# Attention with beacons, then a squared-ReLU feed-forward: fp32 loads and casting transfers at the start, and half products for one more chunk

## The chip, the cores and the metric

The kernel runs on one core of one Trainium2 chip. The metric is the device time of one execution in microseconds (us). Before the change it is 328.27 us, the median of 3 runs that lie between 327.58 and 329.05.

A core has five engines that run their own programs side by side: TensorE (PE; its weight loads are listed apart as PEld), VectorE (DVE), ScalarE (ACT), GpSimd (POOL) and SyncE (SP). SP, ACT and POOL issue transfers here: SP's and ACT's go through hardware queues, POOL's through the software queue, which can also convert fp32 to bf16 on the way.

## The reference

```python
scores = scale * np.matmul(q, k_all.transpose(0, 1, 3, 2))   # k_all = [beacon_k ; k]
scores = np.where(causal, -1000000000.0, scores)             # beacons are always seen
a = np.exp(scores - scores.max(-1, keepdims=True))
a /= a.sum(-1, keepdims=True) + 1e-09
x = np.matmul(a, v_all)                                      # v_all = [beacon_v ; v]
...
h = np.maximum(x @ w_in, 0.0)
return ((h * h) @ w_out).astype(np.float32)
```

There are 8 batches of 8 heads, 576 tokens and 16 beacons for each batch, 64 elements a head. The attention's result, transposed to 4608 tokens of 512, goes through w_in (512 x 2048) and w_out (2048 x 512). Inputs and output are fp32; the kernel computes in bf16 with fp32 sums.

## The kernel before

**Two streams on one TensorE.** Attention runs batch by batch, two heads (a pair) at a time: scores into two wide PSUM strips (names `qk`, line 650), exponentials on ScalarE (`exp`, lines 672 and 748), causal masks on VectorE (`mask`, with the table `tri`), products with v (`av`, line 793), division (`norm`, line 812), and a transpose into xT (`xtp`, `xte`, later `xt` by DMA). The feed-forward runs in nine chunks of 512 tokens, behind the attention: `s1.chunk.part` (line 1095, 512-column matmuls into the PSUM tiles ps), `relu` and `sq` on ScalarE or VectorE, and the second product.

**The second product has two forms.** Chunks 0 and 1 (`j < FAST`, FAST is 2) take the plain one, `s2.chunk.group.quarter` on line 1145: four token groups, four quarters of w_out, 16 matmuls of 512 columns for each group. Chunks from 2 on take the form with seven products on line 1204: the four quadrants of g and of w_out are combined, seven products of halves are made in place of eight (each 2 x 8 matmuls of 256 columns), and VectorE builds sums of quadrants ahead of them (`sum`, line 1176, eight a chunk) and adds the products up behind them (`ev`). Four sums of w_out's quadrants (`wsum`) are made once.

**The order is a table.** SEQUENCE lists every operation by name, with the engine behind an @ where there is a choice (A, D, P). An engine's program is its own operations in the table's order; nothing is reordered when it runs. Buffers (two strips, four ps tiles, six fp32 staging tiles `stg`) are handed out in that order too.

**The start.** Batch 0's tokens 0 to 239 of q and k come in fp32 through hardware queues into osb (`fldq`, `fldk`: pair 0, pair 1, pairs 2 and 3; k's issued by SP, q's by ScalarE) and are cast and paired (`fcq`, `fck`). Its tokens 240 to 575 (part 1) come through the software queue, cast on the way (`sld0..1`, line 474), and VectorE or GpSimd copies two heads side by side (`two0.1.pair`). TensorE transposes pairs (`tp`, line 512), VectorE or ScalarE moves them to qT and kT (`eq`, `ek`, lines 354 and 352). Batch 1's q and k come the same way as part 1 (`sld1`, `two1.0`). The beacon rows of k go through a stg tile (`bkl`, `bkc`). v of batches 0 and 1 comes in fp32 through the software queue into stg (`ld0v`, `ld1v`, line 399) and GpSimd or VectorE casts it to vb (`cast0v`, `cast1v`, line 354). The same queue then carries w_in and w_out in quarters (`win`, line 885; `wout`, line 893), cast on the way. Later batches load q, k and v in fp32 through SP into stg; GpSimd casts.

**Fills.** `fill` is a matmul of the identity with itself (line 486) into a free ps tile; its result is never read. There are 16 of 512 columns, all in the first microseconds or among batch 0's work.

Of the kernel before, what the change touches and what calls it, by code (L numbers as in the profile page):

```python
# [16 lines left out]
fldq2 fcq2@D ld0v3 ident fill6 fill5 fill10 fill15 fldq1 sld0q1.0 fill3 fldq0 sld0k1.0 fill12 fcq3@A fcq1 tp0.0.3q  # L17
eq0.0.3@A tpg0.0.3q fldk1 fck1 tp0.0.1k ek0.0.1@D tpg0.0.1k tri sld0q1.2 tp0.0.2q eq0.0.2@D tpg0.0.2q fill2 fldk2
fill11 fcq0 tp0.0.0q fck2 tp0.0.2k fill4 ek0.0.2@A tpg0.0.2k bkl0 bkc0 tpb0 tp0.0.1q sld0k1.2 fill13 eq0.0.0@A
tpg0.0.0q eq0.0.1@A ekb0 tpg0.0.1q qk2.0.0 exp2.0.0 qk1.0.0 exp1.0.0 two0.1.1q@D tp0.1.1q fck3 tp0.0.3k ek0.0.3@A  # L20
two0.1.0k@D fldk0 fill7 tpg0.0.3k fck0 tp0.0.0k ek0.0.0@A two0.1.1k@D sld1q0.0 tp0.1.1k eq0.1.1@D ek0.1.1@A qk3.0.0
two0.1.0q@D tp0.1.0q tpg0.0.0k qk1.1.1 tpg0.1.1q ld0v0 tp0.1.0k mask1.0.0 ld0v1 tpg0.1.1k fill9 exp3.0.0 ld0v2
exp1.1.1 eq0.1.0@A tpg0.1.0q two0.1.3k@D ek0.1.0@D tpg0.1.0k qk0.0.0 exp0.0.0 sld1k0.2 mask2.0.0 cast0v3 two1.0.1q@D
mask0.0.0 sld1k0.0 qk1.1.0 exp1.1.0 fill8 two0.1.3q@P tp0.1.3q eq0.1.3@D qk0.1.0 ld0v4 qk0.1.2 mask1.1.0 win0
cast0v0@D exp0.1.0 exp0.1.2 tp1.0.1q eq1.0.1@D tpg1.0.1q win1 qk1.1.2 exp1.1.2 tpg0.1.3q cast0v1@P av1.0.0 norm1.0.0
ld1v1 tp0.1.3k qk0.1.1 exp0.1.1 ek0.1.3@A av2.0.0 norm2.0.0 two0.1.2q@P tpg0.1.3k tp0.1.2q mask1.1.1 two0.1.2k@D
tp0.1.2k eq0.1.2@A ek0.1.2@A tpg0.1.2q sld1q0.2 win3 win2 cast0v2 qk3.1.0 exp3.1.0 mask3.0.0 bkl1 bkc1 two1.0.0q@D
tpg0.1.2k av0.0.0 cast0v4 norm0.0.0 qk2.1.0 fill0 av3.0.0 exp2.1.0 xtp0.0.1 xtp0.0.0 qk3.1.1 exp3.1.1 xte0.0.1@D
xte0.0.0@D tpb1 ekb1 fill1 qk3.1.2 norm3.0.0 xtp0.0.2 xte0.0.2@D exp3.1.2 mask0.1.0 mask0.1.1 av1.1.0 norm1.1.0
qk2.1.2 exp2.1.2 mask3.1.1 fill14 tp1.0.0q eq1.0.0@A tpg1.0.0q ld1v3 two1.0.0k@P mask3.1.0 av0.1.0 xtp0.0.3 xte0.0.3@A  # L30
tp1.0.0k qk2.1.1 av3.1.0 norm0.1.0 exp2.1.1 xtp0.1.0 ld1v4 xte0.1.0@A s1.0.0.0 ek1.0.0 tpg1.0.0k qk4.2 relu0.0.0@A
warm wout1 norm3.1.0 mask2.1.0 mask2.1.1 two1.0.1k@P wout3 two1.0.2q@P tp1.0.1k ek1.0.1 tpg1.0.1k exp4.2.1.0.0
s1.0.1.0 relu0.1.0@D xtp0.1.3 av2.1.0 s1.0.2.0 xte0.1.3@D relu0.2.0@D ld2k0 exp4.2.0.0.0 s1.0.4.0 relu0.4.0@D
norm2.1.0 s1.0.3.0 relu0.3.0@A tp1.0.2q eq1.0.2@A tpg1.0.2q xtp0.1.1 xte0.1.1@D qk4.4 xtp0.1.2 xte0.1.2@A s1.0.5.0
relu0.5.0@D two1.0.2k@P tp1.0.2k exp4.4.1.0.0 s1.0.7.0 ek1.0.2 relu0.7.0@A ld1v2 s1.0.6.0 relu0.6.0@A mask4.0.0
tpg1.0.2k sq0.1.0@D s1.0.1.1 relu0.1.1@D ld1v0 cast1v3 s1.0.0.1 two1.0.3k@D exp4.4.0.0.0 mask4.0.2 relu0.0.1@A
s1.0.5.1 relu0.5.1@A s1.0.3.1 relu0.3.1@A qk5.7 exp5.7.-1.1.0 s1.0.15.1 relu0.15.1@A two1.0.3q@P exp5.7.1.0.0
s1.0.12.1 relu0.12.1@D s1.0.4.1 relu0.4.1@D wout0 s1.0.10.0 exp5.7.-1.0.0 s1.0.14.0 relu0.14.0@A s1.0.7.1 relu0.7.1@A
relu0.10.0@D s1.0.2.1 relu0.2.1@A cast1v1 exp5.7.0.0.0 s1.0.15.0 relu0.15.0@D wout2 sq0.7.0@A s1.0.14.1 relu0.14.1@D
s1.0.11.1 relu0.11.1@D sq0.7.1@A s1.0.9.0 relu0.9.0@A s1.0.8.0 s1.0.6.1 s1.0.13.0 relu0.6.1@A mask4.0.1 relu0.8.0@D  # L40
# [12 lines left out]
qk8.4 exp8.4.1.0.0 exp8.4.0.0.0 relu1.9.0@D tr3q st0 s1.1.14.0 relu1.14.0@D tr3k ld3v0 cast3v0 ld3v1 cast3v1 s1.1.13.0
s1.1.2.0 relu1.2.0@A ld3v2 qk8.2 relu1.13.0@D cast3v2 ld3v3 ld3v4 ld4k0 cast3v4 ld4q0 exp8.2.0.0.0 cast4k0
exp8.2.1.0.0 s1.1.15.0 relu1.15.0@D mask8.0.1 mask8.0.0 s1.1.1.0 wsum1 relu1.1.0@A s1.1.3.0 s1.1.7.0 relu1.3.0@A
s1.1.4.0 relu1.4.0@D ld4q1 s1.1.12.0 sq1.1.0@D mask8.0.2 s1.1.0.0 cast4q0 s1.1.6.0 cast3v3 cast4q1 ld4q2 ld4q3 ld4k1
ld4q4 cast4q3 cast4q4 relu1.0.0@A sq1.0.0@D relu1.7.0@A relu1.12.0@D relu1.6.0@A s1.1.8.0 relu1.8.0@A s1.1.5.0
relu1.5.0@D cast4q2 cast4k1 av8.0.0 ld4k2 sq1.3.0@A ld4k3 norm8.0.0 qk9.7 ld4k4 cast4k4 sq1.6.0@A exp9.7.-1.1.0
av8.0.1 norm8.0.1 s1.1.10.0 exp9.7.1.0.0 exp9.7.1.0.1 relu1.10.0@D sq1.2.0@D s1.1.11.0 exp9.7.-1.0.0 s2.1.1.0
mask9.0.0 relu1.11.0@D exp9.7.0.0.0 s2.1.0.0 sq1.4.0@A qk10.10 exp10.10.-1.1.0 exp10.10.0.0.0 exp10.10.1.0.0 mask9.0.2  # L60
sq1.5.0@D exp10.10.-1.0.0 s2.1.1.1 s2.1.0.1 s2.1.1.2 s2.1.0.2 qk11.13 exp11.13.-1.0.0 exp11.13.-1.1.0 cast4k3
sq1.7.0@D s2.1.0.3 mask9.0.1 ev1.0@A s2.1.1.3 s2.1.2.0 ev1.1@A st2 mask10.0.2 mask10.0.1 mask10.0.0 av10.0.0
norm10.0.0 s2.1.2.1 exp11.13.0.0.0 xtp2.0.0 xte2.0.0@A av10.0.1 norm10.0.1 av9.0.0 norm9.0.0 s2.1.2.2 xtp2.0.2 tr4q
# [147 lines left out]
def kernel(  # L211
# [29 lines left out]
    def sb(name, shape, dt):  # L241
        return pool.tile(shape, dt, name=name)

    FAST = 2
    BOTH = 7
    NSTG, NPT, RB = 6, 3, 3
    NFILL = 16
# [1114 lines left out]
```

## Time and profile before

| | before |
|---|---|
| median of 3 runs | 328.27 us |
| the profiled execution | 326.74 us |
| its span, first to last instruction | 325.0 us |
| granted TensorE clock, mean | 0.994 of full speed |
| TensorE instructions | 3428 matmuls, as many weight loads |

The span holds all engines' work; 1.7 us of the execution's time lie outside it. The page of the profile gives each engine's busy time as a share of the span and as a strip of 40 digits, each a slice of 8.1 us (9: busy 90% or more). Views of the trace behind it list groups of equal instructions by source line, waits and what ended them, and single instructions with their start in us from the span's begin. In rows of the kind "29.1, 454 | 0.9 <-PE" stand the busy time of the group, the mean of one in ns, and the idle time of the engine just ahead of them with what ended it.

### The profile page before, as it was taken

How to read it: one execution, taken by the hardware profiler on the slowest of the kernel's cores; microseconds unless marked ns; L12 is line 12 of the kernel's file. 1: busy time of each engine (PE TensorE's matmuls, PEld its weight loads, DVE VectorE, ACT ScalarE, POOL GpSimd, SP SyncE). 2: the span in 40 equal slices, each digit the busy share in tenths (PEclk: the TensorE clock that was granted, in tenths of full speed). 3: DMA queues.
4: the chain of work that ended last, by engine and by line, in shares of the span. 5: the costliest groups of instructions: out<-in, count | busy, mean ns of one | idle time of the engine just before them, and what ended most of it. 6: DMA issues, size and time to landing. Idle time of an engine off the chain costs nothing.

```text
span 325.0 us, 8419 instructions
## 1 busy us (share of the span) xinstructions
PE 314.7 (97%) x3428; PEld 225.4 (69%) x3428; DVE 234.9 (72%) x495; ACT 224.7 (69%) x332; POOL 105.2 (32%) x157
## 2 busy tenths in 40 slices
PE   5889999999999999999999999999999999999995
PEld 2458875645465548878886476657878788888884
DVE  2798493648727888558876778659977597988872
ACT  3897995555867896667765588567874874985920
POOL 8997534327406802422334024413000340000000
PEclk9799999999999999999999999999999999999999
DMA  7999999989999999799988998999520510030033
GB/s 164 213 205 224 230 216 196 184 175 244 217 215 204 222 218 209 144 225 185 206 190 188 205 189 193 169 170 225 125 44 2 141 63 0 2 114 17 3 129 131
DMA packets 145601, 51.97 MB, mean 160 GB/s; under 512 B 132506, under 2 KB 140570, under 8 KB 145562
## 3 DMA queue, kind: packets, MB, share of 16 engines
q1 hardware_dynamic: 135901, 42.32, 63.3%
q0 software_dynamic: 8512, 8.49, 15.2%
q10 hardware_dynamic: 1149, 0.62, 0.8%
q8 instruction: 27, 0.44, 0.6%
q14 instruction: 12, 0.10, 0.1%
HBM read 37.22 MB, written 9.44 MB: 144 GB/s over the span
## 4 chain that ended last, share of the span: by engine, by line
PE 93%; DVE 2%; DMA 2%; issue 1%; ACT 0%; POOL 0%; DVEq 0%; POOLq 0%
PE ps L1095 30%; PE ps L1204 25%; PE ps L793 9%; PE ps L1145 9%; PE strip L650 6%; PE strip L972 4%; PE ps L972 3%; PE strip L1204 2%; PE ps L650 2%; DMA qk_area<-in_q_dram 2%; PE ps L512 1%; PE ps L861 1%; PE ps L486 0%; DVE xn L812 0%; DVE qT L354 0%
## 5 line engine op out<-in xcount | busy, mean ns | idle before, releaser
L1095 PE MATMUL ps<-xT,w_in 128*128 128x512 bf16 (+6 forms) x640 | 104.3, 315 | 0.2 <-issue 0.2
L1095 PEld LDWEIGHTS <-w_in 128*128 128x128 bf16 x640 | 57.2, 98 | 35.4 <-issue 1.7
L748 ACT ACTIVATE pt<-strip 128x1024 bf16<-128x1024 f32 (+3 forms) x77 | 70.2, 952 | 10.1 <-PE strip L650 9.9
L354 POOL CAST qk_area<-stg 128x512 bf16<-128x512 f32 (+2 forms) x60 | 41.2, 712 | 48.7 <-DMA stg<-in_k_dram 24.9
L1110 ACT ACTIVATE g<-ps 128x512 bf16<-128x512 f32 (+2 forms) x74 | 39.0, 551 | 21.7 <-PE ps L1095 18.9
L354 POOL CAST vb<-stg 128x512 bf16<-128x512 f32 (+1 forms) x39 | 27.7, 722 | 76.6 <-DMA stg<-in_v_dram 76.6
L1204 PEld LDWEIGHTS <-g 128*128 128x128 bf16 x448 | 42.7, 98 | 6.7 <-issue 1.1
L1112 DVE TENSOR_SCALAR g<-ps 128x512 bf16<-128x512 f32 (+2 forms) x54 | 32.8, 614 | 20.0 <-PE ps L1095 17.3
L771 DVE TENSOR_TENSOR pt<-pt,tri 128x512 bf16<-128x512 bf16 (+1 forms) x93 | 35.8, 410 | 8.3 <-ACT pt L748 7.9
L793 PEld LDWEIGHTS <-pt 128*128 128x128 bf16 x930 | 34.9, 99 | 6.2 <-issue 1.2
L1204 PE MATMUL ps<-w_out,g 128*128 128x256 bf16 x304 | 38.0, 273 | 0.0
L793 PE MATMUL ps<-vb,pt 128*128 128x65 bf16 x930 | 37.6, 194 | 0.2 <-DVE vb L354 0.2
L1204 PEld LDWEIGHTS <-sum_area 128*128 128x128 bf16 x336 | 31.8, 98 | 5.6 <-issue 1.0
L812 DVE TENSOR_TENSOR xn<-ps,rcp 128x320 bf16<-128x320 f32 (+2 forms) x64 | 31.5, 492 | 2.2
L1120 ACT ACTIVATE g<-g 128x1024 bf16<-128x1024 bf16 (+2 forms) x31 | 28.4, 944 | 5.6 <-DVE g L1112 5.3
L748 ACT ACTIVATE pt<-ps 128x512 bf16<-128x512 f32 x42 | 23.7, 598 | 11.6 <-PE ps L650 11.4
L1145 PE MATMUL ps<-w_out,g 128*128 128x512 bf16 x128 | 31.1, 379 | 0.0
L810 DVE RECIPROCAL rcp<-ps 128x5 f32<-128x5 f32 (+2 forms) x64 | 12.1, 189 | 24.8 <-PE ps L793 24.0
L352 ACT COPY osb<-ps 128x512 f32<-128x512 f32 x24 | 14.1, 590 | 20.9 <-PE ps L1204 16.2
L650 PE MATMUL strip<-qT,kT 64*128 64x128 bf16 (+15 forms) x406 | 27.5, 256 | 0.6 <-ACT pt L672 0.6
L650 PEld LDWEIGHTS <-kT 64*128 64x128 bf16 x520 | 17.5, 95 | 14.2 <-issue 9.4
L1204 PE MATMUL ps<-w_sum,sum_area 128*128 128x256 bf16 x208 | 27.0, 273 | 0.0
(100 smaller groups left out, 383.5 us busy)
## 6 DMA issues: line engine op xcount, KB each, us to landing
out_dram<-osb SPq DMA_DIRECT2D x16, 512.0 KB, 3.9
stg<-in_q_dram SPq DMA_DIRECT2D x24, 256.0 KB, 4.9
stg<-in_k_dram SPq DMA_DIRECT2D x18, 256.0 KB, 4.5
stg<-in_v_dram SPq DMA_DIRECT2D x18, 256.0 KB, 5.6
w_in<-in_moe_w_in_dram POOLq DMA_DIRECT2D x4, 512.0 KB, 12.0
w_out<-in_moe_w_out_dram POOLq DMA_DIRECT2D x4, 512.0 KB, 12.1
stg<-in_v_dram POOLq DMA_DIRECT2D x6, 256.0 KB, 9.1
stg<-in_k_dram SPq DMA_DIRECT2D x6, 224.0 KB, 3.8
```

Of the source, the lines that this page charges most:

```text
L354: eng[e].tensor_copy(dst, src)
L650: nc.tensor.matmul(out, kT[b % 2][hp, pr, 128 * c:128 * c + 128], rhs, start=True, stop=True)
L748: nc.scalar.activation(out, in_, AF.Exp, bias=0.0, scale=scale)
L771: nc.vector.tensor_tensor(out=d, in0=d, in1=tri[0:rows, m0:m0 + m, 0:w][:, None].to_broadcast([rows, 2, m, w]), op=ALU.min)
L793: nc.tensor.matmul(a[0:w, at + (t - tl[0]) * (D + 1):at + (t - tl[0] + 1) * (D + 1)], P[0:rr, hj, o:o + w], vb[b % 2][0:rr, c, 2 * pr + hj ...
L812: nc.vector.tensor_tensor(out=xn[b % 2].rearrange("p t (h d) -> p h t d", d=D)[:, h0:h0 + nh, tl[0]:tl[0] + nt], in0=a[:, :, :, 0:D], in1= ...
L1095: nc.tensor.matmul(h[:, lo - spans[0][0]:hi - spans[0][0]], w_in_sb[:, mc, ft * 128:(ft + 1) * 128], xT[:, mc, lo % RING:lo % RING + hi - lo],
L1110: nc.scalar.activation(dst, h, AF.Relu, bias=0.0, scale=1.0)
L1112: nc.vector.tensor_scalar(out=dst, in0=h, scalar1=0.0, scalar2=None, op0=ALU.max)
L1120: nc.scalar.activation(d, d, AF.Square, bias=0.0, scale=1.0)
L1145: nc.tensor.matmul(o, G[:, fc, ts * 128:(ts + 1) * 128], w_out_sb[:, fc, :], start=(fc == 0), stop=(fc == NFT - 1))
L1204: nc.tensor.matmul(o, lhs[:, f, t * 128:(t + 1) * 128], rhs[:, f], start=fresh and f == 0, stop=f == HF - 1, skip_group_check=True)
```

## The change

- FAST goes from 2 to 1: chunk 1's second product is made by seven half products, with its eight sums; the four `wsum` stand ahead of it in one block.
- Batch 0's part 1 of q and k is loaded in fp32 through hardware queues into stg (`rldk0` by ScalarE, `rldq0`, `rldq2`, `rldk2` by SP). The pairing copies read it there and cast; seven of the eight stand on GpSimd, one on VectorE. All eight of batch 1's stand on GpSimd too.
- v of batches 0 and 1 is cast by the software queue's transfer and lands in vb itself; its staging tiles and its ten casts go (nine on GpSimd, one on VectorE).
- The beacon rows of k land in g[0], and chunk 0's first four relus of each pass wait for their cast.
- Fills: 32 of 256 columns. 19 stand in the start, 4 around the end of chunk 0's first product, 8 in the stretch of chunk 1's second product, 1 near the end.
- `tri` has two tiles in place of four (three were alike).
- SEQUENCE is another order throughout; batch 2's first load stands behind batch 0's pairings.

```diff
-fldq2 fcq2@D ld0v3 ident fill6 fill5 fill10 fill15 fldq1 sld0q1.0 fill3 fldq0 sld0k1.0 fill12 fcq3@A fcq1 tp0.0.3q
...
+bkl0 fldq1 ident tri fill6 fill2 fill1 fill28 fill16 fill15 fill25 ld0v0 bkc0 tpb0 fldk1 bkl1 fck1 tp0.0.1k fill5
+fill4 fldq2 fcq3@D ek0.0.1@D tpg0.0.1k tp0.0.3q fill29 bkc1 ekb0 ld0v1 eq0.0.3@D tpg0.0.3q fcq1 tp0.0.1q eq0.0.1@D
+sld1q0.0 fldq0 fill24 ld0v4 fill27 qk1.0.0 tpg0.0.1q fldk2 fck2 tp0.0.2k fck3 rldk0@A ld0v3 fcq2@A fldk0 ek0.0.2@D
...
-    FAST = 2
+    FAST = 1
...
-    NFILL = 16
+    NFILL = 32
...
-        for i in range(4):
+        for i in range(2):
...
         def emit_load(e):
-            st = stg[ld.held[1]]
+            st = vb[b % 2][:, c, :, 0:D] if soft else stg[ld.held[1]]
...
         ld = add(f"ld{b}{x}{c}", "POOL" if soft else "SP", (1.35 if soft else 1.0) if lo else (0.9 if soft else 0.65), emit_load,
-                 take=("stg", 1), dma=1.2 * rows / 128, behind=[] if soft else load_chain[-1:] + behind, sync=sync)
+                 take=None if soft else ("stg", 1), dma=1.2 * rows / 128, behind=[] if soft else load_chain[-1:] + behind, sync=sync)
...
             load_chain.append(ld)
+        else:
+            cast[b, x, c] = ld
+            return
...
     def add_beacon(b):
+        raw = g[0].rearrange("p f t -> p (f t)")[0:Nb, b * 2 * H * D:(b + 1) * 2 * H * D].bitcast(FP32).rearrange(
+            "p (h d) -> p h d", h=H)
         ld = add(f"bkl{b}", "SP", 0.45, lambda e: [nc.sync.dma_start(
-            out=stg[ld.held[1]][0:Nb], in_=beacon_k[b].transpose([1, 0, 2]))], dma=0.1,
-                 deps=[bk_ev[b - 1]] if b else [], take=("stg", 1))
-        bk = add(f"bkc{b}", "DVE", 0.4, lambda e: nc.vector.tensor_copy(bks[b % 2], stg[ld.held[1]][0:Nb]), deps=[ld], give=ld)
+            out=raw, in_=beacon_k[b].transpose([1, 0, 2]))], dma=0.1)
+        bk = add(f"bkc{b}", "DVE", 0.4, lambda e: nc.vector.tensor_copy(bks[b % 2], raw), deps=[ld] + ([tpb_ops[b - 1]] if b else []))
         cast[b, "bk"] = bk
         box = {}
...
-        box["t"] = add(f"tpb{b}", "PE", 0.2, emit_tp, deps=[bk, ident_op], take=("ps", 1))
+        box["t"] = tpb_ops[b] = add(f"tpb{b}", "PE", 0.2, emit_tp, deps=[bk, ident_op], take=("ps", 1))
...
-    bk_ev = {}
+    bk_ev, tpb_ops = {}, {}
+
+    def raw_part(x):
+        _, np_, ns = parts_of[0][1]
+        n = "qk".index(x) * NSTG // 2
+        return stg_all[0:np_, n:n + NSTG // 2].rearrange("p a b -> p (a b)").rearrange("p (h s d) -> p h s d", h=H, s=ns)
+
+    def add_raw_loads():
+        t0, np_, ns = parts_of[0][1]
+        for lo in range(0, HP, HP // 2):
+            for x, t in (("k", k), ("q", q)):
+                h = slice(2 * lo, 2 * lo + HP)
+
+                def emit(e, t=t, x=x, h=h):
+                    return [eng[e].dma_start(
+                        out=raw_part(x)[:, h],
+                        in_=t[0, h, t0:t0 + np_ * ns, :].rearrange("h (p s) d -> p h s d", s=ns))]
+
+                o = add(f"rld{x}{lo}", ("SP", "ACT"), {"SP": 0.45, "ACT": 0.55}, emit, dma=1.04)
+                for pr in range(lo, lo + HP // 2):
+                    strided[0, 1, pr, x] = o
...
     def add_fill(i):
         def emit(e):
-            nc.tensor.matmul(ps[fill.held[1]], ident, ident[:, None, :].to_broadcast([128, 4, 128]), start=True, stop=True)
-
-        fill = add(f"fill{i}", "PE", 0.216, emit, deps=[ident_op], take=("ps", 1))
+            nc.tensor.matmul(ps[fill.held[1]][:, 0:256], ident, ident[:, None, :].to_broadcast([128, 2, 128]), start=True, stop=True)
+
+        fill = add(f"fill{i}", "PE", 0.108, emit, deps=[ident_op], take=("ps", 1))
         fill.give = [fill]
...
         if b > 0:
-            after = [w_ops["in", 3]] if b == 1 else [strided[b - 1, 0, HP - 1, "q"]]
-            add_part_loads(b, 0, after, free)
+            add_part_loads(b, 0, None, free)
...
                             copy_on(e, paired_buf(b, x, part)[:, pr].rearrange("p s (u d) -> p u s d", u=2),
-                                    strided_buf(b, x, part)[:, 2 * pr:2 * pr + 2])
+                                    (strided_buf(b, x, part) if b else raw_part(x))[:, 2 * pr:2 * pr + 2])
 
                         joined[b, part, pr, xs] = add(f"two{b}.{part}.{pr}{xs}", ("DVE", "POOL"),
-                                                      {"DVE": 0.14 + 2 * ns * D / 3000.0, "POOL": 0.15 + 2 * ns * D / 850.0},
+                                                      {"DVE": 0.14 + 2 * ns * D / (3000.0 if b else 1400.0), "POOL": 0.15 + 2 * ns * D / (1100.0 if b else 850.0)},
                                                       emit_pair, deps=[strided[b, part, pr, xs]])
...
                     relus.append(add(f"relu{j}.{ft}.{n}", ("ACT", "DVE"), {"ACT": 0.17 + N / 1200.0, "DVE": 0.157 + N / 960.0},
-                                     emit_relu, deps=[s1] + (tp_ops[0, 1] if j == 1 else []), give=s1))
+                                     emit_relu, deps=[s1] + (tp_ops[0, 1] if j == 1 else [])
+                                     + ([cast[i, "bk"] for i in range(NPE)] if j == 0 and ft < 4 * NPE // 2 else []), give=s1))
 
...
                 add_fill(i)
-            part_loads = add_part_loads(0, 1, [tri_op], [])
+            add_raw_loads()
...
             behind, sync = [], []
-            if x == "v" and b == 0:
-                if c == 0:
-                    behind = part_loads
-            elif x == "v" and b == 1 and c == 0:
-                behind = [strided[1, 0, HP - 1, "q"]]
-            elif b == 2 and n == 0:
+            if b == 2 and n == 0:
                 sync = [w_ops["out", 3]]
+                behind = [joined[0, 1, pr, y] for pr in range(HP) for y in "kq"]
...
```

Where the table moves things, shown as the instructions of one engine in program order (source line, operation, tile written and tiles read, shape):

**GpSimd, early program, from the loads of batch 0's late q and k to the first weights.** Before:

```order
L474 DMA qk_area<-in_q_dram 112x4x192
L474 DMA qk_area<-in_k_dram 112x4x192
L474 DMA qk_area<-in_q_dram 96x4x384
L398 DMA stg<-in_beacon_v_dram 16x8x64
L399 DMA stg<-in_v_dram 112x8x64
L399 DMA stg<-in_v_dram 128x8x64 x2
L474 DMA qk_area<-in_k_dram 96x4x384
L354 CAST vb_66<-stg 128x8x64
L474 DMA qk_area<-in_k_dram 96x4x384
L354 COPY g_81<-qk_area 112x2x3x64
L399 DMA stg<-in_v_dram 80x8x64
L885 DMA w_in<-in_moe_w_in_dram 128x4x512 x2
```

After:

```order
L399 DMA vb_66<-in_beacon_v_dram 16x8x64
L400 DMA vb_66<-in_v_dram 112x8x64
L400 DMA vb_66<-in_v_dram 128x8x64
L499 DMA qk_area<-in_q_dram 96x4x384
L400 DMA vb_66<-in_v_dram 80x8x64
L400 DMA vb_66<-in_v_dram 128x8x64 x2
L499 DMA qk_area<-in_k_dram 96x4x384
L355 CAST g_81<-stg 112x2x3x64 x2
L909 DMA w_in<-in_moe_w_in_dram 128x4x512
L355 CAST g_81<-stg 112x2x3x64 x4
L355 COPY w_sum<-qk_area 96x2x6x64 x2
L355 CAST g_81<-stg 112x2x3x64
```

The loads of the late q and k have left this engine (rows of 112 partitions on line 474), v is written to vb straight, and the pairings from stg (`two0.1`, written to g_81) stand one behind the other around the first quarter of w_in, with two of batch 1's (written to w_sum) among them.

**ScalarE, among batch 0's exponentials (line 672 before, 696 after; copies on line 352 before, 353 after).** Before:

```order
L672 ACTIVATE pt<-strip_89 128x2x368
L672 ACTIVATE pt<-strip_90 128x2x368
L352 COPY kT_70<-ps_94 128x240
L352 COPY kT_70<-ps_92 128x240
L352 COPY kT_70<-ps_93 128x336
L672 ACTIVATE sum_area<-strip_89 128x2x368
L672 ACTIVATE pt<-strip_90 128x2x416
L352 COPY qT_68<-ps_94 128x336
L672 ACTIVATE pt<-strip_89 128x2x368
```

After, from its first cast of q on:

```order
L353 CAST qk_area<-osb_83 120x2x2x64
L579 DMA osb_83<-in_q_dram 120x2x128
L484 DMA stg<-in_k_dram 112x4x192
L353 CAST qk_area<-osb_83 120x2x2x64 x2
L696 ACTIVATE pt<-strip_89 128x2x368
L353 COPY qT_68<-ps_93 128x240
L353 COPY kT_70<-ps_91 128x240
L696 ACTIVATE pt<-strip_90 128x2x368
L353 COPY kT_70<-ps_91 128x336
L696 ACTIVATE pt<-strip_89 128x2x368
```

The load of pair 0's q and the first fp32 load of the late k are issued by ScalarE behind its first cast and ahead of two more; fewer copies stand between the exponentials.

**TensorE in chunk 1's second product.** Before, where the plain form goes over from one token group (ps_91) to the next (ps_94):

```order
L1145 LDWEIGHTS g_81
L1145 MATMUL ps_91<-w_out,g_81 128x512
L1145 LDWEIGHTS g_81
L1145 MATMUL ps_94<-w_out,g_81 128x512
L1145 LDWEIGHTS g_81
```

After, where fills stand among the half products:

```order
L1229 LDWEIGHTS g_81
L1229 MATMUL ps_91<-w_out,g_81 128x256
L511 LDWEIGHTS ident
L511 MATMUL ps_94<-ident 128x256
L511 LDWEIGHTS ident
L511 MATMUL ps_93<-ident 128x256
L511 LDWEIGHTS ident
L511 MATMUL ps_92<-ident 128x256
L511 LDWEIGHTS ident
L511 MATMUL ps_94<-ident 128x256
L1229 LDWEIGHTS g_81
L1229 MATMUL ps_93<-w_out,g_81 128x256
```

Matmuls of 512 columns have become twice as many of 256 on other operands, and four of the eight fills stand between two of the products.

273 lines of the change are left out of this document (136 added, 137 removed).

## The prediction

> **What bounds the kernel now.** I read the page first, then what TensorE waited for, then stretches of ten microseconds, then the engines inside the one stretch that has idle TensorE time. The page:
>
> ```profile
> span 325.0 us, 8419 instructions
> PE 314.7 (97%) x3428; PEld 225.4 (69%) x3428; DVE 234.9 (72%) x495; ACT 224.7 (69%) x332; POOL 105.2 (32%) x157
> PE   5889999999999999999999999999999999999995
> DMA  7999999989999999799988998999520510030033
> q1 hardware_dynamic: 135901, 42.32, 63.3%
> q0 software_dynamic: 8512, 8.49, 15.2%
> ```
>
> TensorE is busy in every slice but the first three and the last, and the DMA engines are as full as it until two thirds of the span. What TensorE waited for, all of it:
>
> ```profile
> PE ps L486 <- POOL ident masks.py:199: 3.0, 1, 3.0
> PE ps L512 <- DVE g L354: 1.4, 2, 0.9
> PE ps L486 <- ACT qT L352: 0.8, 1, 0.8
> PE strip L650 <- ACT pt L672: 0.6, 2, 0.4
> PE ps L861 <- DVE xn L812: 0.3, 1, 0.3
> PE ps L1095 <- issue: 0.2, 1, 0.2
> PE ps L793 <- DVE vb L354: 0.2, 1, 0.2
> ```
>
> That is 6.5 us, 3.0 of them before the first matmul. Every releaser but "issue" belongs to batch 0 or the start. The stretches agree (columns: length; busy time and instructions of PE, PEld, DVE, ACT, POOL; granted clock; DMA share; GB/s):
>
> ```profile
> 10.00:20.00 10.00, 7.80 (x85) 4.50 (x85) 8.79 (x24) 9.57 (x16) 10.00 (x14) 0.83 1.29 219
> 30.00:40.00 10.00, 10.00 (x121) 8.39 (x118) 5.83 (x17) 8.24 (x18) 7.13 (x11) 1.00 1.22 227
> ```
>
> So there are two places where time can be won: the first 27 us, in which ScalarE (9.57 of 10) and GpSimd (10.00) are full and TensorE is not, and, from 30 us on, TensorE's own work. A third fact limits the first: the DMA share is above 1 in both stretches, so a transfer that becomes dearer moves all behind it.
>
> **Part 1, half products for chunk 1.** The 64 matmuls of 128x512 on line 1145 become 7 products of 16 matmuls of 128x256. From the chain of waits, a run of each:
>
> ```profile
> 83.49 1.73 PE ps L1145 x8
> 123.37 1.75 PE ps L1204 x16
> ```
>
> 64 x 0.216 = 13.8 us go and 112 x 0.109 = 12.2 us come: -1.6 us, on the engine that is the bound. Vector work comes with it: eight sums, each like these:
>
> ```profile
> L1176 DVE TENSOR_TENSOR sum_area<-g x14: 680/693/950, 116.9 to 308.6; 128x1024 bf16<-128x1024 bf16 x14
> ```
>
> That is 8 x 0.69 = 5.5 us of VectorE, and four weight sums brought forward into one block. VectorE is 72% busy, and chunks 2 to 6 carry the same sums with no TensorE wait, so I cost them at nothing; if that cover fails, TensorE waits for a sum of 0.7 us, and for a chain of two before product 6, 1.4. The order shows that it is not quite covered: between the scores qk10.10 and qk12.5 TensorE now gets eight fill matmuls of 256 columns, which stand where plain products stood, because product 6 needs sums and the next scores need the exponentials of the last. Filled or idle, that is time: 8 x 0.109 = +0.9. Four more fills stand around the end of chunk 0's first product: +0.4. Together part 1 and its fills are -0.3.
>
> **Part 2, batch 0's late q/k and the new start.** What ends the start is ScalarE's run of 16 exponentials, from its first to its last:
>
> ```profile
> 9.69 1.46 ACT L672 ACTIVATE pt<-strip 128x736 bf16<-128x736 f32 x2 [0.32 <-PE strip L650]
> 26.59 0.86 ACT L672 ACTIVATE pt<-strip 128x832 bf16<-128x832 f32 x1 [0.19 <-PE strip L650]
> ...
> L672 ACT ACTIVATE pt<-strip 128x832 bf16<-128x832 f32 (+2 forms) x12 | 9.7, 872 | 0.9 <-PE strip L650 0.8
> L672 ACT ACTIVATE sum_area<-strip 128x832 bf16<-128x832 f32 (+2 forms) x4 | 3.4, 866 | 0.4 <-PE strip L650 0.4
> L352 ACT COPY kT<-ps 128x336 bf16<-128x336 bf16 (+1 forms) x5 | 2.1, 418 | 0.4 <-PE ps L512 0.3
> L352 ACT COPY qT<-ps 128x336 bf16<-128x336 bf16 (+1 forms) x3 | 1.6, 528 | 0.0
> L352 ACT COPY xT<-ps 128x240 bf16<-128x240 bf16 x1 | 0.4, 359 | 0.0
> ```
>
> Nine copies (4.1 us) stand among the exponentials now. In the new order six do: two of 240, three of 336, one of 576 columns, 2 x 0.36 + 3 x 0.46 + 0.63 = 2.7. So -1.4. The others go to VectorE, which loses six pairings (two0.1), two of batch 1 and one cast of v to GpSimd or to the transfer. Against it, the first exponential starts later: q of pair 0 is now issued by ScalarE behind its first cast.
>
> ```profile
> 4.86 0.40 ACT L352 CAST qk_area<-osb 120x256 bf16<-120x256 f32 x1 [1.21 <-DMA osb<-in_q_dram]
> osb<-in_q_dram ACTq DMA_DIRECT2D x2, 120.0 KB, 5.5
> ```
>
> Issued near 5 and landing 4 to 5.5 later, cast by 9.5 to 11: 0 to +1.3, I take +0.7. Then TensorE has done more when the exponentials end. The first scores of batch 1 follow them:
>
> ```profile
> 27.39 0.57 PE L1095 MATMUL ps<-xT,w_in 128*128 128x240 bf16 x4
> 27.89 0.56 PE L650 MATMUL strip<-qT,kT 64*128 64x512 bf16 x6
> ```
>
> In the new order one more such group of line 1095 (0.5 us) and two small transposes (0.4) come ahead of those scores: -0.9. Sum of part 2: -1.4 + 0.7 - 0.9 = -1.6. Bounds: -2.3 if q lands at once; 0 if ScalarE idles 1.6 us more than the 1.7 in the idle column, waiting for GpSimd's seven pairings, which now run one behind the other from the landing of pair 0 and 1's late k.
>
> **Part 3, the price of the transfers.** By the two queue rows, q1 took 63.3% x 325 x 16 = 3292 us for 42.32 MB, or 4.9 us of all 16 engines per MB; q0 took 790 us for 8.49 MB written, 5.8 us per MB. A late q/k load (112 partitions x 4 heads) is 0.34 MB in fp32 on a hardware queue, 1.7 us by q1, against 0.17 MB written by q0, 1.0: 0 to +0.7 each. q1's mean packet is 311 bytes and these runs have 768, so I take +0.27 each, +1.1 for four.
>
> A tile of v (128 rows) in fp32 by the software queue, read behind a quarter of w_in:
>
> ```profile
> 14.97 1.51 POOL L885 DMA_DIRECT2D w_in<-in_moe_w_in_dram  x2
> w_in<-in_moe_w_in_dram POOLq DMA_DIRECT2D x1, 512.0 KB, 11.4
> 17.20 0.90 POOL L399 DMA_DIRECT2D stg<-in_v_dram  x1
> stg<-in_v_dram POOLq DMA_DIRECT2D x1, 256.0 KB, 10.8
> ```
>
> The second quarter, issued at 15.7, lands at 27.1, v at 28.0: 0.9 us for the tile; by q0's pace it would be 1.5; I call it 1.1. The same tile cast by the transfer writes half the bytes, 0.76 by q0's pace, but in 1024 runs of 128 bytes, 64 for each engine. If each run costs a packet as q1's do (3292 us / 135901 = 24.2 ns), that is 1.55. No row shows such a transfer; the nearest one has the same queue and the same 256-byte source runs, so I take 1.1, no change, and keep 0.76 to 1.55. There are 9.25 tiles (1152 rows and two beacons): -3.1 to +4.2 us of DMA, 0 taken. The Trainium skill, "DMA: Bandwidth & Descriptors", section Specifications, speaks against the change: transfers below 512 bytes cost a read-modify-write. No row here shows that; if it made the 128-byte runs as dear as q1's packets, the sum below would be that of the slower rival.
>
> What this moves is the last quarter of w_out:
>
> ```profile
> L893 POOL DMA_DIRECT2D w_out<-in_moe_w_out_dram x4: 748/766/782, 24.7 to 38.5; - x4
> w_out<-in_moe_w_out_dram POOLq DMA_DIRECT2D x1, 512.0 KB, 10.4
> 46.95 1.89 PE L1145 MATMUL ps<-w_out,g 128*128 128x512 bf16 x8
> 49.54 3.20 PE L1145 MATMUL ps<-w_out,g 128*128 128x512 bf16 x14
> ```
>
> It lands at 38.5 + 10.4 = 48.9. Its first reader is the ninth matmul of the second group, 49.54 + 8 x 0.216 = 51.3, so 2.4 us of slack. In the new order the same amount of TensorE work stands ahead of the first reader, so it is wanted at 51.3 - 1.6 + 0.2 (two fills) = 49.9 and lands at 48.9 + 1.1 = 50.0: a wait of 0.1. The slack is used up exactly; every 0.1 us per tile of v beyond 1.1 is 0.9 us of TensorE.
>
> GpSimd itself sheds nine casts of v and two of the four masks, and takes eight more pairings; it is waited for only through the pairings of part 2. The casts of v and their buffers go, and batch 2's loads then find six free slots: off the path, nothing.
>
> **Sum.** -1.6 (half products) + 0.9 + 0.4 (fills) - 1.6 (start) + 0.1 (w_out) = -1.8 us. The profiled execution took 326.7 (span 325.0 and 1.7 around it), 1.5 below the median of the runs; I take the difference from the median: 328.3 - 1.8 = 326.5.
>
> **Rivals.** *w_out late (slower).* Mechanism: the 128-byte runs. Place: chunk 0's second product, first group on the last quarter. At 1.55 per tile the quarter lands 4.2 later and all of it is waited for: 328.3 - 1.8 + 4.2 = 330.7. It is slower than before beyond 0.5% (1.6 us, about what a measurement of this kernel tells from no change) from 1.1 + 3.4 / 9.25 = 1.47 per tile. For it: DMA share above 1 and no slack left. Against: the same source runs, half the bytes.
>
> *The start gains nothing.* GpSimd's pairings or the late q of pair 0 hold ScalarE back. Then w_out is not waited for, and what is left is -0.3: 328.0. The same time comes from v at 1.3 per tile (+1.8). For it: the pairings all wait behind one landing on one engine. Against: ScalarE has 1.4 us less to do.
>
> *Half products blocked by VectorE.* The chain of two sums before product 6 uncovered: +1.4 on the forecast, 327.9; counted with the second.
>
> **Chances.** Forecast 0.50, start without gain (or v at 1.3) 0.27, w_out late 0.23. Of the forecast's half, 0.06 falls within 0.5%, since -1.8 is close to the bound; 0.02 of the second falls below it. Faster 0.46, same 0.31, slower 0.23. Range: from the part 2 bound (-2.3) with cheap v (the wait gone) and half the fills free, -4 or so, 324.0, to the slow rival's 330.6. The forecast's own range is 324.5 to 328.
>
> **What would show it.** ScalarE's last exponential of batch 0 ending near 26.5 (right) or after 27.5 (start wrong). TensorE's list of waits naming a DMA of w_out on the line of the second product (slower rival), or nothing of the kind. The interval between landings of v tiles against 1.1. Idle time of TensorE between the scores of chunk 1's stretch, beyond the eight fills (sums uncovered). Fewer matmul microseconds on chunk 1's second product by 1.6. If waits of TensorE appear after 100 us, the new order itself is worse and the forecast is wrong for a reason not priced here.

## The result and the profile after

The changed kernel takes 330.35 us (median of 20 runs, 327.42 to 334.39), the kernel before 328.13 in the same runs (20, 326.43 to 329.75). The ratio is 1.0067, interval 1.0043 to 1.0091: about 2.2 us slower, where 1.8 us faster was forecast. Ratios here leave disturbed runs out, so they aren't the quotient of the medians. The profiled execution took 330.11, 3.4 more than that of before. Its page:

```profile
span 328.4 us, 8531 instructions
PE 316.3 (96%) x3474; PEld 233.5 (71%) x3492; DVE 244.3 (74%) x518; ACT 212.0 (65%) x311; POOL 97.9 (30%) x150
PE   5899999999999999999979999999999999999995
PEclk9999999999999999999998999999999999999999
DMA  8999999989989999988989998699421600030042
q1 hardware_dynamic: 137293, 43.35, 64.2%
q0 software_dynamic: 15488, 6.59, 17.5%
```

Of the weak digits of the start one has gone (the third slice), but a 7 stands in the 21st slice, 164 to 172 us, with an 8 in the clock behind it. What TensorE waited for, the five longest:

```profile
PE ps L817 <- POOL vb L355: 2.0, 1, 2.0
PE ps L511 <- POOL ident masks.py:199: 1.4, 1, 1.4
PE ps L536 <- DVE qk_area L355: 1.4, 2, 1.2
PE ps L536 <- POOL g L355: 0.6, 1, 0.6
PE ps L536 <- ACT qk_area L353: 0.6, 1, 0.6
```

The longest wait is new and late: the product with v (line 817) waits 2.0 us for a cast to vb on GpSimd. In stretches (columns as in the prediction):

```profile
10.00:20.00 10.00, 9.19 (x98) 5.10 (x97) 7.19 (x22) 7.92 (x12) 7.01 (x12) 1.00 1.68 203
170.00:173.00 3.00, 1.01 (x18) 0.84 (x17) 0.00 (x0) 1.78 (x3) 2.62 (x5) 0.86 0.64 140
173.00:177.00 4.00, 4.00 (x44) 3.09 (x41) 1.22 (x4) 0.00 (x0) 1.45 (x3) 0.68 0.98 208
177.00:181.00 4.00, 3.95 (x24) 2.02 (x22) 3.24 (x7) 2.71 (x4) 1.36 (x2) 1.00 0.87 223
```

From 10 to 20 us TensorE is busy 9.19 at clock 1.00, where before it was 7.80 at 0.83. The granted clock is 0.86 from 170 to 173 and 0.68 from 173 to 177: 3 x 0.14 + 4 x 0.32 = 1.7 us lost, most of it behind the wait of 2.0. The kernel before lost as much between 10 and 20 us (10 x 0.17 = 1.7), so the clock does not explain the 3.4 us between the two profiled executions. By the pages TensorE idles 12.1 us (328.4 - 316.3) against 10.3, and is busy 1.6 longer. Why the cast was late stands on GpSimd's own timeline:

```profile
161.71 1.65 POOL L355 CAST vb<-stg 128x512 bf16<-128x512 f32 x2 [1.13 <-DMA stg<-in_v_dram]
163.30 0.61 POOL L355 CAST qk_area<-stg 128x512 bf16<-128x512 f32 x1
170.38 1.17 POOL L355 CAST qk_area<-stg 128x512 bf16<-128x512 f32 x2 [6.47 <-DMA stg<-in_q_dram]
171.50 0.61 POOL L355 CAST vb<-stg 128x512 bf16<-128x512 f32 x1
```

The cast at 171.50 is batch 5's first tile of v (`cast5v0`). In the new table it stands behind `cast6q3` and `cast6q2`, and GpSimd stands 6.47 us before the first of these, for the last of four loads that SP issued here:

```profile
158.47 2.58 SPq L868 DMA_TRANSPOSE xT<-xn  x1
161.14 0.53 SPq L1158 DMA_DIRECT2D out_dram<-osb  x1
161.78 4.81 SPq L400 DMA_DIRECT2D stg<-in_q_dram  x4
166.68 3.46 SPq L868 DMA_TRANSPOSE xT<-xn  x2
```

Before, four of that v's five casts stood ahead of batch 6's, and the fifth behind one of them.

### The profile page after: what moved, and what is told of

The parts are those of the page before. It is cut to its first block, busy times and chain, and to the rows that moved or that the text cites. A ratio compares the mean times of both kernels' runs of the same rounds, so it can differ in the third digit from the quotient of the medians.

```text
span 328.4 us, 8531 instructions
## 1 busy us (share of the span) xinstructions
PE 316.3 (96%) x3474; PEld 233.5 (71%) x3492; DVE 244.3 (74%) x518; ACT 212.0 (65%) x311; POOL 97.9 (30%) x150
## 3 DMA queue, kind: packets, MB, share of 16 engines
q1 hardware_dynamic: 137293, 43.35, 64.2%
q0 software_dynamic: 15488, 6.59, 17.5%
## 4 chain that ended last, share of the span: by engine, by line
PE 83%; DMA 7%; DVE 4%; SPq 2%; issue 2%; POOL 1%; ACT 0%; POOLq 0%; DVEq 0%
PE ps L1119 26%; PE ps L1229 25%; PE ps L817 8%; PE strip L674 5%; PE strip L996 4%; PE ps L1170 4%; PE ps L996 3%; DMA stg<-in_k_dram 2%; PE strip L1229 2%; DMA stg<-in_v_dram 2%; PE ps L674 2%; DMA stg<-in_q_dram 1%; PE ps L885 1%; SPq L437 1%; DVE pt L795 1%
## 5 line engine op out<-in xcount | busy, mean ns | idle before, releaser
L1229 PEld LDWEIGHTS <-g 128*128 128x128 bf16 x512 | 48.4, 98 | 8.9 <-issue 2.2
L1136 DVE TENSOR_SCALAR g<-ps 128x512 bf16<-128x512 f32 (+2 forms) x56 | 33.7, 611 | 16.2 <-PE ps L1119 15.6
L1229 PE MATMUL ps<-w_out,g 128*128 128x256 bf16 x352 | 44.1, 273 | 0.0
L355 POOL CAST vb<-stg 128x512 bf16<-128x512 f32 (+1 forms) x30 | 20.5, 702 | 70.4 <-DMA stg<-in_v_dram 59.5
L1229 PEld LDWEIGHTS <-sum_area 128*128 128x128 bf16 x384 | 36.9, 99 | 6.3 <-issue 0.6
L795 DVE TENSOR_TENSOR pt<-pt,tri 128x512 bf16<-128x512 bf16 (+1 forms) x93 | 36.5, 420 | 5.8 <-ACT pt L772 4.8
L1229 PE MATMUL ps<-w_sum,sum_area 128*128 128x256 bf16 x240 | 31.1, 273 | 0.0
L674 PE MATMUL strip<-qT,kT 64*128 64x128 bf16 (+15 forms) x406 | 28.4, 261 | 0.1
L1252 DVE TENSOR_TENSOR osb<-ps,osb 128x512 f32<-128x512 f32 (+1 forms) x26 | 16.7, 647 | 14.6 <-PE ps L1229 8.6
L834 DVE RECIPROCAL rcp<-ps 128x5 f32<-128x5 f32 (+2 forms) x64 | 12.1, 189 | 18.9 <-PE ps L817 17.2
```

The costliest lines, as they stand in the source:

```text
L355: eng[e].tensor_copy(dst, src)
L674: nc.tensor.matmul(out, kT[b % 2][hp, pr, 128 * c:128 * c + 128], rhs, start=True, stop=True)
L795: nc.vector.tensor_tensor(out=d, in0=d, in1=tri[0:rows, min(m0, 1):(2 if m0 else m), 0:w][:, None].to_broadcast([rows, 2, m, w]), op=ALU.min)
L1136: nc.vector.tensor_scalar(out=dst, in0=h, scalar1=0.0, scalar2=None, op0=ALU.max)
L1229: nc.tensor.matmul(o, lhs[:, f, t * 128:(t + 1) * 128], rhs[:, f], start=fresh and f == 0, stop=f == HF - 1, skip_group_check=True)
```

## The experiments

Each is timed against the kernel before on its chip, in 6 to 12 runs:

| run | median, us | ratio to before | interval |
|---|---|---|---|
| head_only | 327.79 | 0.9997 | 0.9966 to 1.0028 |
| tail_only | 330.76 | 1.0061 | 1.0020 to 1.0103 |
| v_cast_early | 330.62 | 1.0045 | 1.0004 to 1.0085 |
| v_cast_early_no_late_fills | 331.13 | 1.0108 | 1.0046 to 1.0170 |
| v_and_xT_early | 330.12 | 1.0091 | 1.0048 to 1.0134 |
| store_behind_loads | 330.03 | 1.0039 | 1.0006 to 1.0071 |
| late_compute_new | 327.43 | 0.9965 | 0.9938 to 0.9992 |
| late_transfers_new | 332.80 | 1.0103 | 1.0067 to 1.0140 |
| late_pool_order_new | 333.59 | 1.0175 | 1.0125 to 1.0225 |
| late_sp_order_new | 331.22 | 1.0037 | 0.9994 to 1.0080 |
| late_casts_in_load_order | 329.57 | 1.0047 | 1.0008 to 1.0086 |
| start_only | 328.33 | 1.0028 | 0.9990 to 1.0065 |
| half_only | 328.17 | 1.0020 | 0.9989 to 1.0050 |
| head_no_late_fills | 328.40 | 0.9998 | 0.9962 to 1.0035 |
| best_no_late_fills | 329.07 | 1.0012 | 0.9974 to 1.0050 |
| head_pairs_on_vector | 329.49 | 1.0046 | 1.0017 to 1.0076 |
| best_copies_on_vector | 327.76 | 0.9980 | 0.9949 to 1.0010 |
| best_store_early | 328.07 | 1.0006 | 0.9971 to 1.0042 |

The order is a table, so a kernel can be grafted: the rows of one table up to a place, then all that is left in the order of the other. The cut lies in chunk 2's first product, near 110 us.

**Which part loses.** Head new and tail old, then the reverse:

```diff
 head_only: table of the change up to ld5k0
+then every operation left, in the order of before
 tail_only: table and code of before up to exp13.8.1.0.0
+then every operation left, in the order of the change
```

> The new order up to chunk 2's first product (start, transfers, half products, fills), then the order of before for all that is left. Theory L (the loss is one wait late in the new order, GpSimd's cast of a tile of batch 5's v standing behind casts of batch 6's q): no wait of TensorE after 100 us, and -1.6 for half products, +1.3 for fills, 0 for the start, so 0.1 to 0.8 us below before, 327.3 to 328.0. Rival S (the loss is the start and its transfers, which make everything after them late): about as the changed kernel, 330.4, with a wait after 150 us again.

> The order and code of before up to chunk 2's first product, then the new order for all that is left. Theory L: TensorE waits about 2 us for GpSimd's cast to vb near 165 us, and the granted clock falls behind it, in all +2.5 to +3.8, so 330.6 to 331.9. Rival S: nothing late arrives, so 328.1, as before.

The head alone can't be told from before (0.9997), and the 1.8 us of the forecast, 0.55%, lie outside its interval; the tail alone costs what the change costs (1.0061). The wait for vb that was expected of tail_only is not shown, though: its profiled execution took 328.14, where its executions lie between 327.39 and 333.81, and TensorE's waits in it behind 100 us come to 0.9 us, none of them for vb. All the named parts of the change, loads, casting transfers, half products and all fills but one, are in the head. The loss is in the order of what they left alone.

**One word moved.** The late cast, then more:

```diff
 v_cast_early:
-... cast6q3 cast6q2 ... sum3.4.0 cast5v0 qk20.5
+... cast5v0 cast5v2 cast5v1 ...
 v_cast_early_no_late_fills: the same, and
-fill20 fill30 fill10 fill14 fill26 fill0 fill19 fill18 fill22 fill31 fill7 fill9
 v_and_xT_early: cast5v0 as above, and
-xt4.0 ... ld6k1 ld6q4 ld6k2 ... xt4.2
+xt4.0 xt4.2 ... ld6k1 ld6q4 ld6k2
 store_behind_loads: both of these, and
-st5 ... ld6q0 ld6q1 ld6q2
+ld6q0 ld6q1 ld6q2 st5
```

> The changed kernel with one word of the order moved: the cast of batch 5's first v tile stands first among that batch's v casts, no longer behind two casts of batch 6's q. Theory L: the wait of 2.0 us and the dip of the clock behind it go, 2.2 to 3.7 us below the changed kernel, 326.7 to 328.1. Rival S: the cast was late because its buffers and transfers are late, the wait moves to the next cast or load, less than 1 us gained, 329.5 or more.

> The kernel with the early cast, without the 12 fills in chunk 0's and chunk 1's second products. If TensorE's work behind them could have started earlier: 1.3 us below it, 325.4 to 326.8. If they only fill waits for exponentials and sums: same as it within 0.3, with waits of 1.3 us listed in their place. If a pause lets the granted clock fall: above it by 0.5 or more.

> The changed kernel with two words of the order moved: batch 5's first v cast ahead of the others, and the transfer of batch 4's third piece to xT (the one chunk 4's first product starts on) ahead of three loads of batch 6 on SP. Theory L2 (the new order lets batch 6's loads hold up whatever stands behind them on GpSimd and SP; with the cast moved, the piece of xT is what came late, 3.1 us in one profile): both gone, as the kernel with the new order up to chunk 2 alone, 327.3 to 328.3. Rival: the loss wanders on to a third place, 330 or more.

> The changed kernel with three words moved: the v cast and the piece of xT as before in this study, and the store of chunk 2's lower half behind three loads of batch 6's q on SP, which it stood ahead of (in the profile SP stood 2.7 us before that store, and the loads behind it). Theory Q with this place as its cause: 327.3 to 328.4. Rival: the slack is thin in several places, another one is caught, 329.5 or more.

All four stay slower than before, and by the intervals none can be told from the changed kernel. In their profiles the wait for vb is gone, and others have come, some at a piece of xT that the first product of a chunk starts on, or at an evacuation to osb (a product moved out of PSUM). Lines of TensorE's waits behind 100 us, of the run without late fills, the run with two words moved and the one with three:

```profile
PE ps L1118 <- DMA xT<-xn: 3.1, 1, 3.1
```

```profile
PE ps L1119 <- DMA xT<-xn: 1.0, 1, 1.0
```

```profile
PE ps L1229 <- DVE osb L355: 1.8, 2, 0.9
PE ps L1119 <- DMA xT<-xn: 1.1, 2, 0.9
```

So my first theory, one late cast, fell: the cast was one of several places with too little slack.

**Transfers or computing.** From the cut on, each engine's own order is kept whole, but for a few transfers near the end, and taken from different tables (the staging tiles are handed out anew in the merged order):

```diff
 from chunk 2's first product on                SP      GpSimd   TensorE, VectorE, ScalarE
 the changed kernel                             new     new      new
+late_compute_new                               old     old      new
+late_transfers_new                             new     new      old
+late_pool_order_new                            old     new      new
+late_sp_order_new                              new     old      new
```

> The changed kernel, but from chunk 2's first product on SP and GpSimd (loads, casts, transposes by transfer, stores) run in the order of before; TensorE, VectorE and ScalarE keep the new order. Theory Q (the late loss is in the new order of the transfer queues): as the new order up to chunk 2 alone, 327.2 to 328.4, no wait over 1 us after 120 us. Rival C (the new order of the computing engines asks for things earlier or ties them up): 330 or more.

> The other half: from chunk 2's first product on SP and GpSimd keep the new order, TensorE, VectorE and ScalarE run in the order of before. Theory Q: the loss is here, 330 to 331. Rival C: 327.2 to 328.4. If both halves are slow or both fast, it takes the two together.

> The changed kernel, but from chunk 2's first product on SP runs in the order of before, GpSimd in the new order. If the order of the casts on GpSimd carries the loss (a v cast behind q casts): 1% above before, 330.5 or more. If SP's does: at or below before.

> The changed kernel, but from chunk 2's first product on GpSimd runs in the order of before, SP in the new order. If SP's order of loads, transposes and stores carries the loss: 1% above before. If GpSimd's does: at or below before. Above before by about half in both: each takes a share.

With the old transfers the new head is at 0.9997 (old computing order) and 0.9965 (new); with the new ones at 1.0103 and 1.0067. The intervals of the two pairs don't meet: the order on SP and GpSimd costs about 1%, whatever the other engines do, and the new order of the computing engines is itself no worse. How that divides between the two queues isn't told: GpSimd's new order alone gives 1.0175, more than the changed kernel with both, so two orders that don't match cost something themselves; SP's alone is not settled (0.9994 to 1.0080). The profile of late_transfers_new shows the wait of the changed kernel again; that of late_pool_order_new another one, for an evacuation of chunk 3 on ScalarE:

```profile
PE ps L817 <- POOL vb L355: 1.9, 1, 1.9
```

```profile
PE ps L1229 <- ACT osb L353: 5.0, 2, 3.7
```

In the same trace ScalarE's evacuation waits 4.67 us for a store:

```profile
173.24 0.59 ACT L353 COPY osb<-ps 128x512 f32<-128x512 f32 x1 [4.67 <-DMA out_dram<-osb]
```

By the program that is chunk 2's store, which stands on SP behind loads; these need tiles that GpSimd gives back. The profile of late_compute_new, which was expected to have no wait over 1 us, has a shorter one of this kind, 1.7. late_casts_in_load_order asks whether GpSimd's order is bad because casts stand out of the order of their loads:

```diff
-cast5v2 cast5v1 cast5v3 cast5v4 cast6k0 cast6q3 cast6q2 cast5v0 cast6q0 cast6q1 cast6q4
+cast5v0 cast5v1 cast5v2 cast5v3 cast5v4 cast6k0 cast6q0 cast6q1 cast6q2 cast6q3 cast6k1
```

> The changed kernel with one thing changed: from chunk 2's first product on GpSimd's casts stand in the order in which SP issues their loads. If casts out of the order of their loads carry the loss: 0.6 to 1.0% below the changed kernel, at 0.0 to 0.3% above or below before. If the transfers are late for another reason (the stores and transposes on SP): still 0.5 to 1% above before.

It is at 1.0047, inside the range of neither outcome alone. The wait for vb is gone from its profile, one for xT is there:

```profile
PE ps L1119 <- DMA xT<-xn: 1.7, 2, 1.5
```

**The parts of the head.** start_only has the new start and chunk 0, with FAST left at 2 (and four more fills behind chunk 0, about 0.4 us by the prediction's 0.109 each); half_only the old code and start with chunk 1's half products and no fill among them; head_no_late_fills is head_only without 12 fills.

```diff
 start_only: table of the change to the end of chunk 0, then that of before
-    FAST = 1
+    FAST = 2
 half_only: table of before to chunk 1, that of the change to chunk 2, that of before
-    FAST = 2
+    FAST = 1
```

> The new start, transfers and chunk 0 (FAST left at 2: chunk 1's second product plain), then the order of before. If the start gains nothing and four fills cost 0.4: 0.0 to 0.5 above before, 327.7 to 328.6. If the start gains the 1.6 of the prediction: 326.9 or less. If the transfers are dearer and w_out comes late: 329 or more, with a wait for w_out on the line of the plain second product.

> The code and start of before, chunk 1 in the new order with its seven half products and no fill among them, then the order of before. If TensorE's shorter work counts in full: 1.6 below before, 326.1. If 0.9 of it is idle time for exponentials and sums, which the fills only covered: 0.7 below, 327.0. If a pause of TensorE lets the clock fall: same as before or slower.

> The new order up to chunk 2 without the 12 fills in the two second products, then the order of before. If the fills stand in time in which TensorE could work: 0.8 to 1.3 below the same kernel with them, 326.5 to 327.2 and about 0.3% below before. If they cover waits: 327.5 to 328.2.

None of the three can be told from before. best_no_late_fills (late_compute_new without the 12 fills) showed no gain either:

> The new order of the computing engines with the late transfers in the order of before, without the 12 fills in the two second products. If the fills stand in time TensorE could use: 0.2 to 0.4% below the same with fills, which was 0.35% below before, so 0.55 to 0.75% below before. If they cover waits: 0.2 to 0.4% below before.

**Copies on GpSimd against masks on VectorE.** In the start of the changed kernel GpSimd pairs batch 1's k, from 20.98 on, and VectorE masks from 20.98 on. First GpSimd's row, then VectorE's:

```profile
20.98 1.80 POOL L355 COPY w_sum<-qk_area 96x768 bf16<-96x768 bf16 x2
```

```profile
20.98 1.90 DVE L795 TENSOR_TENSOR pt<-pt,tri 128x512 bf16<-128x512 bf16 x2
```

Two masks take 1.90 us, as long as the copies beside them. The runs move these copies:

```diff
 head_pairs_on_vector (head_only, and pair 2's too), at the places they had
-two1.0.1k@P two1.0.0k@P
+two1.0.1k@D two1.0.0k@D
 best_copies_on_vector (best_no_late_fills)
-two1.0.1k@P ... two1.0.0k@P
+norm1.1.0 two1.0.1k@D ... norm0.1.0 two1.0.0k@D
 best_store_early: best_copies_on_vector, and
-ld6q2 ld6q3 ... st5
+st5 ld6q2 ld6q3
```

> The new order up to chunk 2, then that of before, with four of batch 1's pairing copies (pair 0 and 1's k, pair 2's k and q) on VectorE in place of GpSimd. Theory P (VectorE's masks stand still while GpSimd copies bf16 to bf16: two masks took 1.9 us over such a copy, 0.41 each elsewhere, and one 1.12): the masks take 0.4 again and the start ends 0.7 to 1.5 earlier, 326.3 to 327.1. Rival: the masks were not on the path, 327.6 to 328.

> The kernel without late fills, with two of batch 1's pairing copies (pair 0's and 1's k) on VectorE, each right behind a division there and not at the place they had on GpSimd. Theory P: the two masks take 0.56 in place of 1.9, VectorE wins 0.7 over, the start ends 0.3 to 0.7 earlier: 0.1 to 0.2% below the run without late fills. Rival: the masks aren't waited for, the same as it within 0.1%.

> The kernel without late fills and with two copies on VectorE, with the store of chunk 2's lower half ahead of two loads of batch 6's q on SP. If the evacuation that waited for that store (0.8 to 5.0 us in four profiles) is what is left: 0.3 to 0.6% below before. If not: as the kernel without this move, 0.2% below.

In best_copies_on_vector GpSimd only issues transfers in that stretch, and VectorE's row reads:

```profile
20.98 0.56 DVE L795 TENSOR_TENSOR pt<-pt,tri 128x512 bf16<-128x512 bf16 x2
```

That the copies hold up the masks is shown: 1.90 to 0.56 us. In head_pairs_on_vector, with four copies on VectorE, TensorE waits 1.4 us for them, and it lost (1.0046). In the better place ScalarE's last exponentials of batch 0 begin at 25.31, against 26.20 in the profile of best_no_late_fills. The times, 0.9980 and 1.0012, have intervals that overlap, so a gain in the total isn't shown. best_store_early brought nothing.

The best version is late_compute_new, 0.35% below before (interval 0.08 to 0.62) and clear of the changed kernel. It is the lowest of 18 runs, and its nearest relatives, head_only (0.9997) and best_no_late_fills (1.0012), are not below before, so a gain over before is not established.

## Why the prediction was wrong

**The step that failed.** The sum priced the new order at two places, the start and chunk 1, and put nothing for the rest of the table; the late order came in only as a last sentence, that waits after 100 us would make it "itself worse". That is what happened: +1.0% from the order of SP and GpSimd behind 110 us; in the profiled execution it shows as 2.0 us of wait with a fall of the clock behind it. Between the forecast of -1.8 and the measured +2.2 lie 4.0 us: tail_only's 0.61% is 2.0 of them, and 1.7 are the gain that head_only lacks (-0.1 in place of -1.8), which the next paragraphs take up; the rest is within the intervals. One place could have been read in the order, `cast5v0` behind two casts of later loads, but moving it alone did not bring the time back. What exactly makes the late order of the two queues dear stays open. Four edits of single places and the casts in load order took the wait for vb out of the profiles, others stood in its place, and the time stayed. That all of them hang on one chain, casts that give back tiles, loads that need them, and stores and pieces of xT behind those loads on SP, is argued from the profiles and the program, not shown.

**Half products and fills: -0.3.** Not seen in the time. TensorE's work did shrink: chunk 1's second product keeps it busy for 14.4 us in place of 15.5, 1.1 less where 1.6 was forecast. But half_only, by the prediction's terms 0.7 us (0.2%) below before, is between 0.1% below and 0.5% above; where the saved time goes is open. The sums weren't waited for in the changed kernel's profile, as forecast. That the fills' time would be idle without them ("Filled or idle, that is time") isn't borne out: in chunk 1's stretch (80 to 114 us) TensorE waits 0.3 us in the profile of best_no_late_fills and not at all in that of head_no_late_fills. Yet in none of three pairs is the kernel without late fills the faster one, and none differs beyond its intervals, so what the fills cost stays open too.

**The start: -1.6.** Wrong; the rival "the start gains nothing" held. ScalarE's exponentials of batch 0, first and last:

```profile
8.40 0.78 ACT L696 ACTIVATE pt<-strip 128x736 bf16<-128x736 f32 x1
...
25.98 1.70 ACT L696 ACTIVATE pt<-strip 128x832 bf16<-128x832 f32 x2
```

They begin at 8.40, 1.3 earlier than before and not 0.7 later, so that term had the wrong sign. But they end at 27.68, past the 27.5 that the prediction named as the sign of a failed start, against 27.45 before. ScalarE's groups from 8.3 to 27.7, as the prediction has them of before:

```profile
L696 ACT ACTIVATE pt<-strip 128x832 bf16<-128x832 f32 (+2 forms) x12 | 10.1, 863 | 1.0 <-PE strip L674 0.6
L696 ACT ACTIVATE sum_area<-strip 128x832 bf16<-128x832 f32 (+2 forms) x4 | 3.5, 867 | 0.9 <-PE strip L674 0.9
L353 ACT COPY kT<-ps 128x336 bf16<-128x336 bf16 (+1 forms) x4 | 1.7, 416 | 1.9 <-PE ps L536 1.9
L353 ACT COPY qT<-ps 128x240 bf16<-128x240 bf16 (+1 forms) x2 | 1.0, 492 | 0.0
```

The six copies cost 2.7 us, as forecast. ScalarE's idle time came to 3.8 in place of 1.7, past the 1.6 more at which the prediction's bound puts the gain at 0. Of it 1.9 stand before 13 us, ahead of two copies of kT; ahead of the second TensorE waits 0.6 for a pairing on GpSimd, the mechanism of the rival. Later ScalarE waits for scores. One wrong step here was that GpSimd "is waited for only through the pairings of part 2": its copies also hold up VectorE, and the masks are on the way from the exponentials to the products with v. The Trainium skill states this, in "SBUF — State Buffer", section Who interferes with whom: a VectorE instruction with two inputs from SBUF and a GpSimd instruction that reads SBUF exclude each other, and the later one stands until the other has ended. The masks have two such inputs, and the trace agrees (1.90 us beside copies of 1.80); weighed against the eight added pairings it would have spoken against part 2. How much of ScalarE's later idle time comes from the masks isn't measured by itself; with two copies moved the last exponentials began 0.9 earlier, in one profile each.

**The transfers and w_out: +0.1, rival 330.7.** The rival's time, 330.7, came near the result by luck, since its mechanism is not what happened: the only list of waits that names w_out is best_store_early's, with 0.3 us. The last quarter of w_in and the last full piece of v, both with their time to landing, and the last quarter of w_out:

```profile
w_in<-in_moe_w_in_dram POOLq DMA_DIRECT2D x1, 512.0 KB, 10.0
vb<-in_v_dram POOLq DMA_DIRECT2D x1, 112.0 KB, 9.5
```

```profile
24.37 0.77 POOL L909 DMA_DIRECT2D w_in<-in_moe_w_in_dram  x1
29.90 0.84 POOL L400 DMA_DIRECT2D vb<-in_v_dram  x1
36.21 0.74 POOL L917 DMA_DIRECT2D w_out<-in_moe_w_out_dram  x1 [0.80 <-DMA vb<-in_v_dram]
```

```profile
w_out<-in_moe_w_out_dram POOLq DMA_DIRECT2D x1, 512.0 KB, 13.2
```

Between 24.4 + 10.0 and 29.9 + 9.5, 464 rows of v land in 5.0 us: 1.4 a tile of 128, where 1.1 was taken and 1.47 was the point from which the rival decides. w_out lands at 36.2 + 13.2 = 49.4, not at the 50.0 of the prediction, and beside 48.9 before: the term of 1.1 came to 0.5 although a tile was dearer than taken, and nothing waited in the changed kernel. With 1.4 a tile the prediction's sum would have had the quarter 9.25 x 0.3 = 2.8 later still; which term makes up for it isn't told. The queue rows, from which the prices were made, don't show it: the packets of both queues took 13 us more of all 16 engines than before ((64.2 + 17.5)% of 328.4 against (63.3 + 15.2)% of 325.0).

**The range.** Its lower end doesn't follow from its own terms: -1.6 (half products) - 2.3 (the start at its best) + 0.65 (half the fills) is -3.3, not -4. Nothing hangs on it.

## What to carry to other kernels

When an order is rewritten as a whole, price it queue by queue to the end, transfers first: for each late consumer ask what stands ahead of its cast, its load and its store on their in-order queues, since TensorE can be full everywhere and still lose to a few late tiles. A wait found in one profile is one draw: grafting whole orders, one group of engines at a time, told in two runs what four edits of single places did not. Work moved to GpSimd isn't free for VectorE, even where nothing waits for GpSimd.

## What the runs showed of the hardware

The granted clock falls behind some pauses of TensorE and not others. After 2.0 us of idle time it was 0.68 from 173 to 177 us in the changed kernel; in late_pool_order_new the stretches at and behind its pause read

```profile
170.00:174.00 4.00, 0.31 (x5) 0.20 (x2) 0.14 (x1) 0.76 (x2) 2.02 (x4) 0.83 0.93 203
174.00:178.00 4.00, 4.00 (x31) 3.06 (x30) 2.09 (x6) 2.71 (x5) 0.83 (x2) 0.50 0.65 139
```

while the pause of 3.1 us in v_cast_early_no_late_fills left it whole:

```profile
172.00:175.50 3.50, 0.53 (x10) 0.27 (x10) 1.98 (x4) 1.94 (x2) 2.19 (x5) 1.00 1.16 205
175.50:179.00 3.50, 3.36 (x15) 1.59 (x17) 1.65 (x3) 0.60 (x1) 1.59 (x3) 1.00 0.89 229
```

and so did the pause of 1.9 us in late_transfers_new, at the same place in the program as the one of 2.0:

```profile
171.00:173.50 2.50, 0.60 (x18) 0.46 (x15) 0.12 (x1) 1.75 (x3) 2.25 (x5) 1.00 0.68 153
173.50:177.00 3.50, 3.32 (x48) 2.53 (x47) 2.69 (x7) 0.53 (x1) 1.81 (x4) 1.00 0.96 208
```

The Trainium skill, "TensorE: Matmul & The Clock Gate", Part 1, has the clock halved after an idle window of about 3.4 us, and the windows run freely. The pause of 2.0 us is shorter than that, and the measurement decides: such a pause can cost 1.7 us more, or nothing.

Executions of one kernel differ by more than the effects sought: 29 of the kernel before, on one chip, lay between 326.05 and 330.54 us. With 12 runs half a per cent is about what can be told.
